# A recurrent attention layer and a routed feed-forward layer in one kernel: gates of the first 256 steps ahead, routing cut into small pieces, weights and q loaded in other portions

## The chip, the core and the metric

The kernel runs on one core of a Trainium2 chip. The core has five engines that each work through an instruction list of their own: TensorE (PE in the rows; its weight loads are PEld), VectorE (DVE), ScalarE (ACT), GpSimd (POOL) and SyncE (SP), which here only issues DMAs. The lists are joined by semaphores. SBUF is the on-chip memory, PSUM takes the results of the matrix unit. The metric is the time of one execution on the device in microseconds (us), as the median of repeated runs.

## The reference

Two layers stand one behind the other. The first is an mLSTM cell with an exponential input gate, which the reference runs step by step:

```python
for t in range(S):                         # B, H, S, D = 4, 8, 768, 40
    m_new = np.maximum(f_gate[:, :, t] + m, i_gate[:, :, t])
    f_stab = np.exp(f_gate[:, :, t] + m - m_new)
    i_stab = np.exp(i_gate[:, :, t] - m_new)
    m = m_new
    C = f_stab * C + i_stab * (v_t outer k_t)      # D x D
    n = f_stab * n + i_stab * k_t
    y[:, :, t] = sigmoid(o_gate[:, :, t]) * (C @ q_t) / max(|n . q_t|, 1)
```

Its rows become a table of 3072 rows of 320 numbers. The second layer sends each row to one of 8 experts, chosen by its token number alone (`token * 2654435761 % 8`), and computes `relu(x @ w1[e]) @ w2[e]` with 1024 hidden units. All numbers are f32.

## The kernel before

**Attention.** The 768 steps of a batch are six blocks of 128 steps. One pass of the main loop is one block of one batch: pass `s` is block `c = s % 6` of batch `b = s // 6`, 24 passes in all (called passes here, to keep them apart from the reference's steps). A prologue computes the gates of all steps of all batches: a running maximum over the 768 steps (`gates`, one scan), then decays within each block, each split into three bf16 pieces, written to a DRAM scratch table and read back per block: `load_a(s)` brings the decay pieces into one of two tiles `R`, `load_e(b)` the input pieces of a whole batch into one of two tiles `L`. A pass then does, on TensorE, in this order:

- `turn_k(s + 2)`: transposes k of the pass after the next (L285); `turn_q(b + 1, r)`: transposes sixths of q of the NEXT batch (L301): one sixth at c = 0, two at c = 1, one each at c = 2, 3, 4, none at c = 5, none in the last batch. ahead of each, `pad_q` copies that sixth into a padded tile `qp` on VectorE (L293)
- `decays(s + 1)`: outer sums of gate pieces (`ab` L316, `xb` L324), which ScalarE turns into weights `w` by Exp
- `state(s)` (L382), `scores(s + 1)` (`sp`, L353), which VectorE multiplies into `w` (L357)
- `attend(s)`: rows of the output in `xh` (L396 with the carried state `C`, L401 with `w`). VectorE then takes the denominators `den`; the next pass multiplies them with the output gate on GpSimd (`gated`, `og`), finishes the rows (`finish`, `x`) and stores them

SP issues the loads of a pass ahead of it: k and v of three passes ahead, `load_a(s + 2)`, the output gates, q of a whole batch at once (`load_q`, tile `ql`, 960 KB), and the store of x, which waits for VectorE in the middle of a pass. SP's list is worked off in order, so what stands behind a wait is late too.

**Routing.** Ranks and slots of the tokens per expert need VectorE, a little TensorE and GpSimd. They are independent of the attention and are spread over it by a dictionary: `pieces[s]` runs at the end of pass s, behind `attend(s)`. `route_slots` is one piece (after pass 5), and `route_table` makes one-hot tables of six token columns on VectorE (`oh_c`, `oh_r`) and GpSimd and at once multiplies them on TensorE (`tk`, L544), after passes 6 to 9. `load_weights(e)` of the first three experts (2.5 MB each) are pieces too, after passes 12, 14 and 16.

**Experts.** When the last row is stored, GpSimd gathers rows by expert (L629), TensorE transposes them (L649, L651) and runs layer 1 (L666, L673) and layer 2 (L702) of each expert in turn; outputs are scattered to DRAM. The weights of expert e + 3 are loaded behind expert e.

## Time and profile before

| | |
|---|---|
| median of 3 runs | 499.65 us (499.44 to 501.44) |
| profiled execution | 499.33 us, of which the span of the core is 497.6 us |
| mean granted TensorE clock in the span | 0.912 of full speed |
| TensorE, VectorE, ScalarE, GpSimd busy | 421.3, 148.7, 129.8, 112.1 us |

The profiled execution lies 0.3 us below the median. Its span is the time from the first to the last recorded instruction; some 1.7 us lie around it. A busy time is a mean over a prologue, 24 passes and 8 experts, which are limited by different things, so the table alone doesn't tell what an edit is worth. In the rows a time in square brackets is the idle time of that engine just before the instruction, and the name behind the arrow is what ended it. SPq and ACTq rows are DMA issues by SP and ScalarE. The granted clock is given as a share of 2.4 GHz: 1.00 is that level throughout, 0.5 would be 1.2 GHz throughout.

### The profile page before, as it was taken

The numbers are of one execution on the slowest core, as the hardware profiler recorded it, in microseconds if no ns is written. First come the engines' busy times: TensorE is split into PE (matmuls) and PEld (weight loads), VectorE is DVE, ScalarE is ACT, GpSimd is POOL, SyncE is SP. The second block draws the span as 40 slices with busy tenths as digits, with TensorE's granted clock in tenths as the row PEclk, the third lists the DMA queues.
The fourth block names the chain that finished last, engine by engine and source line by source line (L and its number), as shares of the span: only waits on it lengthen the run. The fifth ranks groups of instructions, "written<-read, shape, count | busy, mean of one in ns | idle before, by whom it ended". The sixth has DMA issues, their size and how long they took to land.

```text
span 497.6 us, 6769 instructions
## 1 busy us (share of the span) xinstructions
PE 421.3 (85%) x2604; PEld 297.2 (60%) x2604; DVE 148.7 (30%) x379; ACT 129.8 (26%) x221; POOL 112.1 (23%) x176
## 2 busy tenths in 40 slices
PE   0288885888895789799399999999999999999993
PEld 0167773777784678688156656565565656656552
DVE  6525657444463354365211020201102011110100
ACT  4795541121442444133011111111111111111100
POOL 3106211222212221142521402313122131102011
PEclk9999976677787898799589999999999999999997
DMA  7374447222346988731314417271331710001000
GB/s 183 78 168 85 98 81 178 42 43 44 68 95 177 240 251 234 176 73 41 90 55 135 143 23 228 67 235 56 119 125 51 232 60 13 26 0 39 1 13 28
DMA packets 103642, 50.94 MB, mean 102 GB/s; under 512 B 79572, under 2 KB 99896, under 8 KB 103608
## 3 DMA queue, kind: packets, MB, share of 16 engines
q1 hardware_dynamic: 100392, 41.59, 32.8%
q0 software_dynamic: 2496, 8.20, 5.2%
q10 hardware_dynamic: 720, 0.70, 0.5%
q8 instruction: 21, 0.34, 0.3%
q14 instruction: 13, 0.11, 0.1%
HBM read 42.07 MB, written 8.63 MB: 102 GB/s over the span
## 4 chain that ended last, share of the span: by engine, by line
PE 69%; issue 10%; DMA 8%; DVE 6%; POOL 3%; ACT 2%; SPq 1%; POOLq 0%; ACTq 0%; DVEq 0%
PE mh L673 19%; PE zp L702 18%; PE mh L666 5%; PE xh L401 5%; PE sp L353 4%; PE xh L396 3%; PE ab L316 3%; PE tr L301 3%; DMA R<-gate_pieces 2%; PE xh L382 2%; PE tk L544 2%; PE tr L285 2%; DMA k<-in_k_dram 2%; DMA ql<-in_q_dram 1%; PE tp L649 1%
## 5 line engine op out<-in xcount | busy, mean ns | idle before, releaser
L702 PE MATMUL zp<-w2t,h 128*128 128x320 f32 x384 | 105.2, 433 | 0.0
L673 PE MATMUL mh<-xT,w1t 128*128 128x416 f32 x256 | 98.2, 528 | 0.9 <-issue 0.9
L702 PEld LDWEIGHTS zp<-w2t,h 128*128 128x128 f32 x384 | 72.7, 190 | 32.1 <-issue 3.3
L673 PEld LDWEIGHTS mh<-xT,w1t 128*128 128x128 f32 x256 | 47.6, 194 | 43.9 <-issue 42.8
L401 PE MATMUL xh<-v,w 128*128 128x41 f32 x384 | 54.1, 275 | 0.0
L655 DVE COPY xT<-tp 128x384 f32<-128x384 f32 x16 | 8.9, 557 | 141.7 <-PE tp L651 124.0
L401 PEld LDWEIGHTS xh<-v,w 128*128 128x128 f32 x384 | 49.8, 193 | 0.7 <-issue 0.4
L636 POOL DMA_INDIRECT out_dram<-zo,s_idx x26 | 25.6, 985 | 92.6 <-ACT zo L635 92.6
L682 ACT ACTIVATE h<-mh 128x416 f32<-128x416 f32 x32 | 16.5, 517 | 109.5 <-PE mh L666 59.6
L286 ACT COPY kT<-tr 128x512 f32<-128x512 f32 x24 | 14.0, 584 | 101.9 <-PE tr L285 101.9
L635 ACT COPY zo<-zp 128x320 f32<-128x320 f32 x26 | 11.1, 425 | 101.1 <-PE zp L702 92.9
L301 PE MATMUL tr<-ident,qp 128*128 128x128 f32 x96 | 20.9, 368 | 17.0 <-DVE qp L293 15.0
L680 DVE TENSOR_SCALAR h<-mh 128x416 f32<-128x416 f32 x32 | 18.9, 591 | 53.4 <-PE mh L673 26.9
L396 PE MATMUL xh<-C,qs 128*128 128x82 f32 x160 | 34.7, 299 | 0.0
L357 DVE TENSOR_TENSOR w<-sp,w 128x512 f32<-128x512 f32 x48 | 30.8, 683 | 11.1 <-PE sp L353 9.7
L353 PE MATMUL sp<-qT,kT 64*128 64x128 f32 x384 | 32.3, 315 | 0.0
L302 ACT COPY qT<-tr 128x512 f32<-128x512 f32 x24 | 25.2, 1092 | 17.6 <-PE tr L301 17.6
L413 POOL TENSOR_TENSOR og<-og,den 128x320 f32<-128x320 f32 x24 | 17.4, 724 | 54.6 <-DVE den L410 43.8
L353 PEld LDWEIGHTS sp<-qT,kT 64*128 64x128 f32 x384 | 27.5, 217 | 2.9 <-issue 0.4
L301 PEld LDWEIGHTS tr<-ident,qp 128*128 128x128 f32 x96 | 14.9, 186 | 21.1 <-issue 16.9
L328 DVE TENSOR_TENSOR qs<-qT,xb 128x512 f32<-128x512 f32 x20 | 13.8, 688 | 44.5 <-PE xb L324 44.5
L666 PE MATMUL mh<-xT,w1c 64*128 64x416 f32 x128 | 26.7, 535 | 0.0
(158 smaller groups left out, 429.1 us busy)
## 6 DMA issues: line engine op xcount, KB each, us to landing
w2t<-in_moe_w_dram SPq DMA_DIRECT2D x8, 1280.0 KB
w1t<-in_moe_w_dram SPq DMA_DIRECT2D x8, 1024.0 KB
ql<-in_q_dram SPq DMA_DIRECT2D x4, 960.0 KB
k<-in_k_dram SPq DMA_DIRECT2D x24, 160.0 KB
v<-in_v_dram SPq DMA_DIRECT2D x24, 160.0 KB
og<-in_o_gate_dram SPq DMA_DIRECT2D x24, 160.0 KB
x_rows<-x SPq DMA_DIRECT2D x24, 160.0 KB
w1c<-in_moe_w_dram SPq DMA_DIRECT2D x16, 128.0 KB
```

Of the source, the lines that this page charges most:

```text
L301: nc.tensor.transpose(tp[:, j, :], t[:, 2 * j : 2 * j + 2, :].rearrange("p h d -> p (h d)"), ident[:])
L302: nc.scalar.copy(qb[b]["T"][:, :, r::NB], tp[:])
L353: nc.tensor.matmul(sp[hf][:, j, :], lhsT=d["kT"][r, j, :], rhs=q_of(s)[r, j, :], start=True, stop=True,)
L357: nc.vector.tensor_tensor(d["w"][:, hf], sp[hf][:], d["w"][:, hf], op=ALU.mult)
L396: nc.tensor.matmul(d["xh"][:, 2 * j * D1 : (2 * j + 2) * D1], lhsT=d["qs"][:, j, :], rhs=st["C"][:, j].rearrange("p h d -> p (h d)"), star ...
L401: nc.tensor.matmul(hs[:, 2 * j + hf, :], lhsT=d["w"][:, hf, j, :], rhs=d["v"][:, 2 * j + hf, :], start=(c == 0), stop=True, skip_group_che ...
L413: nc.gpsimd.tensor_tensor(og[s], og[s], st[s]["den"][:].to_broadcast([P, H, D]), op=ALU.mult)
L636: ins = nc.gpsimd.indirect_dma_start(out=out[:, :], out_offset=bass.IndirectOffsetOnAxis(ap=idx, axis=0), in_=zo[:], in_offset=None, bound ...
L666: nc.tensor.matmul(hp[i][:, :cols], lhsT=w1c[r, fp, :], rhs=xT[r, 2, :cols], start=first, stop=not first,)
L673: nc.tensor.matmul(hp[i][:, :cols], lhsT=w1t[:, db, fb * P : (fb + 1) * P], rhs=xT[:, db, :cols], start=(first and db == 0), stop=(not fir ...
L680: nc.vector.tensor_relu(h[:, 2 * fp, :cols], hp[i][:, :cols])
L702: nc.tensor.matmul(zp[:], lhsT=h[:, fb, j * P : (j + 1) * P], rhs=w[2][:, fb, :], start=(fb == 0), stop=(fb == FB - 1),)
```

## The change

- **Gates in two parts.** The first 256 steps (32 rows, blocks 0 and 1 of every batch) are computed straight from the first third of the scan, without the copy into the layout `mP`; the other 512 steps (64 rows) behind the scores of pass 0. `gates` writes the decay and input pieces, `gates_rest` the exponentials. Each now writes two scratch tables, `za_d` and `ze_d`, on SP. Part of the copies is on GpSimd.
- **Tables.** Only one `R` and one `L` are built; the other of each pair is filled by a DMA from the first, ahead of `load_a(0)` and `load_e(0)`.
- **q.** q of batch 0 is loaded by blocks (`load_q0`, 160 KB each), two in the prologue, the rest in passes 0 to 2, and transposed in the prologue and passes 0 to 3. `load_q(1)` is issued in pass 0. For the other batches `pad_q` for the next pass stands at the end of a pass, ahead of `attend`, in four tiles `qp` instead of two.
- **Routing.** The work is cut into pieces of one to five VectorE instructions that stand ahead of `attend` in passes 2 to 19; the one-hot tables are of three columns, made a pass ahead of their matmuls.
- **Weights.** Ten DMAs per expert; those of experts 0 and 1 go one per pass in passes 3 to 12 and 13 to 22, expert 2 is loaded when the gathers are issued.
- **Order of the loads in a pass.** k, (q), R, v, (L), (q of a batch), output gates, weight slice; R used to be behind v.

```diff
-    wpool = ctx.enter_context(tc.tile_pool(name="wpool", bufs=3))
-    w2pools = [ctx.enter_context(tc.tile_pool(name="w2pool", bufs=3))]
+    wpools = [ctx.enter_context(tc.tile_pool(name="wpool", bufs=2))]
+    w2pools = [ctx.enter_context(tc.tile_pool(name="w2pool", bufs=2))]
...
+        parts = [
+            (t[:, db, f0 : f0 + F // 2], s1[:, db, f0 : f0 + F // 2])
+            for t in (w1t,) for db in range(2) for f0 in (0, F // 2)
+        ]
+        parts += [(w1c[i * P // 2 : (i + 1) * P // 2], last[i]) for i in range(2)]
+        parts += [(w2t[:, fb : fb + 2, :], s2[:, fb : fb + 2, :]) for fb in range(0, FB, 2)]
+        return (w1t, w1c, w2t), [lambda d=d, r=r: nc.sync.dma_start(d, r) for d, r in parts]
...
+    def weight_slices(e):
+        W[e], slices = weights(moe_w1[e], moe_w2[e], wpools[e % 3 // 2], w2pools[2 <= e < 6])
+        return slices
...
-        qps = [gp.tile([P, H, DP], F32, name=f"qp{i}") for i in range(2)]
+        qps = [gp.tile([P, H, DP], F32, name=f"qp{i}") for i in range(4)]
...
+        def load_k(s):
+            st[s] = {"k": ks[s % NK], "v": vs[s % NK]}
+            nc.sync.dma_start(ks[s % NK][:, :, :D], rows_of(k, s))
+        def load_v(s):
+            nc.sync.dma_start(vs[s % NK][:, :, :D], rows_of(v, s))
...
+        def load_e(b, gs):
+            src = ze_d.rearrange("(g b h) i t -> b (h i) g t", g=NC2, h=H)[b]
+            nc.sync.dma_start(
+                Ls[b % 2][: 3 * H, :].rearrange("r (g t) -> r g t", t=W2)[:, gs[0] : gs[-1] + 1],
+                src[:, gs[0] : gs[-1] + 1],
+            )
...
+        def gates(rows, m0, m1, f, i, engs):
+            r = rows
+            first = r.start == 0
+            nc.vector.tensor_add(aP[r], f, m0)
+            nc.vector.tensor_sub(aP[r], aP[r], m1)
+            if first:
+                nc.vector.memset(aP[r, 0:1], 0.0)
+            nc.gpsimd.tensor_tensor(iP[r], i, m1, op=ALU.subtract)
+            nc.vector.tensor_tensor_scan(AP[r], keep[r], aP[r], 0.0, op0=ALU.mult, op1=ALU.add)
+            def copies(z, i0, t, ra, rb, eng):
+                for j, piece in enumerate((hi(t[r]), hi(ra[r]), rb[r])):
+                    (eng.copy if eng is nc.scalar else eng.tensor_copy)(z[r, i0 + j, :], piece)
+            nc.vector.tensor_tensor(r1[r], AP[r], hi(AP[r]), op=ALU.subtract)
+            nc.vector.tensor_sub(iP[r], iP[r], AP[r])
+            nc.vector.tensor_tensor(r2[r], r1[r], hi(r1[r]), op=ALU.subtract)
+            copies(zA, 0, AP, r1, r2, engs[0])
+            nc.vector.tensor_tensor(r3[r], iP[r], hi(iP[r]), op=ALU.subtract)
+            nc.vector.tensor_tensor(r4[r], r3[r], hi(r3[r]), op=ALU.subtract)
+            copies(zE, 0, iP, r3, r4, engs[1])
+            zr = slice(0, BH) if first else slice(BH, 3 * BH)
+            nc.sync.dma_start(za_d[zr, :3, :], zA[r, :3, :])
+            nc.sync.dma_start(ze_d[zr], zE[r])
...
+        def gates_rest(rows, eng):
+            r = rows
+            first = r.start == 0
+            zr = slice(0, BH) if first else slice(BH, 3 * BH)
...
+            nc.scalar.activation(aP[r], aP[r], AF.Exp)
+            nc.scalar.activation(fP[r], AP[r], AF.Exp)
...
+            for j, piece in enumerate((hi(fP[r]), hi(r1[r]), r2[r])):
+                (eng.copy if eng is nc.scalar else eng.tensor_copy)(zA[r, 3 + j, :], piece)
+            nc.sync.dma_start(za_d[zr, 3:, :], zA[r, 3:, :])
...
+            t = qb[b][r] = qps[2 + r % 2]
...
+        def load_q0(c):
+            t = qb.setdefault(0, {})[c] = qps[c % 2]
+            nc.sync.dma_start(t[:, :, :D], rows_of(q, c))
+        def turn_q0(c):
+            turn_q(0, c, slice(c * P, (c + 1) * P))
...
-        pieces = {
-            1: [route_consts], 3: [route_counts], 4: [route_extra], 5: [route_slots],
-            6: [lambda: route_table(0)], 7: [lambda: route_table(1)], 8: [lambda: route_table(2)],
-            9: [lambda: route_table(3)], 10: [route_index],
-            12: [lambda: load_weights(0)], 14: [lambda: load_weights(1)], 16: [lambda: load_weights(2)],
+        before = {
+            0: [lambda: iota_consts(0, 3)], 1: [lambda: iota_consts(3, 8)], 2: [route_consts, route_sel],
+            3: [route_ranks], 5: [route_extra1], 6: [route_extra2], 7: [route_rank],
+            8: [lambda: route_beyond(NM, rmoff)], 9: [lambda: route_beyond(CAP, b2)], 10: [route_slots],
+            11: [route_split], **{12 + i: [lambda i=i: route_hot(i)] for i in range(NT // TH)},
         }
+        after = {4: [route_counts], **{13 + i: [lambda i=i: route_table(i)] for i in range(NT // TH)}}
+        after[12 + NT // TH].append(route_index)
...
+        load_k(0)
+        load_q0(0)
+        load_k(1)
+        load_q0(1)
...
+        g0, g1 = slice(0, BH), slice(2 * BH, 4 * BH)
+        nc.vector.tensor_tensor_scan(
+            m_sb[:, 1 : W2 + 1], f_sb[:, :W2], i_sb[:, :W2], NEG, op0=ALU.add, op1=ALU.max,
+        )
+        turn_k(0)
+        turn_q0(0)
+        turn_k(1)
+        turn_q0(1)
+        gates(g0, m_sb[:, :W2], m_sb[:, 1 : W2 + 1], f_sb[:, :W2], i_sb[:, :W2], (nc.gpsimd, nc.scalar))
+        nc.sync.dma_start(Rs[1][:], Rs[0][:])
+        nc.sync.dma_start(Ls[1][:], Ls[0][:])
         load_a(0)
-        load_e(0)
-        load(2)
-        for r in range(NB):
-            pad_q(0, r)
-            turn_q(0, r)
+        load_e(0, [0])
...
+        for i, eng in ((1, nc.scalar), (2, nc.scalar)):
+            for t, src in ((fP, f_gate), (iP, i_gate)):
+                eng.dma_start(t[at[i] : at[i] + BH, :], src.rearrange("b h s -> (b h) s")[:, i * W2 : (i + 1) * W2])
+        nc.vector.tensor_tensor_scan(
+            m_sb[:, W2 + 1 :], f_sb[:, W2:], i_sb[:, W2:], m_sb[:, W2 : W2 + 1], op0=ALU.add, op1=ALU.max,
+        )
+        for i in (1, 2):
+            nc.scalar.dma_start(mP[at[i] : at[i] + BH, :], m_sb[:, i * W2 : (i + 1) * W2 + 1])
+        gates_rest(g0, nc.gpsimd)
         nc.scalar.dma_start(tok[:], moe_token_ids.rearrange("(p t) -> p t", t=NT))
-        turn_k(0)
-        turn_k(1)
+        load_k(2)
+        load_q0(2)
+        load_v(1)
         load_a(1)
-        load_q(1)
+        for s in range(3):
+            load_o(s)
+        load_v(2)
         decays(0)
         k_weights(0)
+        scores(0)
         sigmoid(0)
-        scores(0)
+        gates(g1, mP[g1, :W2], mP[g1, 1:], fP[g1], iP[g1], (nc.gpsimd, nc.scalar))
+        gates_rest(g1, nc.gpsimd)
+        load_e(0, [1, 2])
...
+        slices = []
         for s in range(NT):
             b, c = s // NB, s % NB
             if s + 3 < NT:
-                load(s + 3)
+                load_k(s + 3)
+                if b == 0 and c < 3:
+                    load_q0(c + 3)
             if s + 2 < NT:
                 load_a(s + 2)
+            if s + 3 < NT:
+                load_v(s + 3)
+            if c == 3 and b + 1 < B:
+                load_e(b + 1, [0, 1, 2])
+            if s == 0:
+                load_q(1)
+            if c == 5 and b + 2 < B:
+                load_q(b + 2)
...
+            if s in (3, 13):
+                slices += weight_slices(s // 10)
+            if slices:
+                slices.pop(0)()
...
+            if b == 0 and c < 4:
+                turn_q0(c + 2)
             if b + 1 < B:
                 for r in turns_of.get(c, ()):
-                    pad_q(b + 1, r)
-                    turn_q(b + 1, r)
+                    if r not in qb[b + 1]:
+                        pad_q(b + 1, r)
+                    turn_q(b + 1, r, slice(r, None, NB))
...
+            nb = b + (c == NB - 1)
+            if nb + 1 < B and s + 1 < NT:
+                for r in turns_of.get((c + 1) % NB, ()):
+                    pad_q(nb + 1, r)
+            for piece in before.get(s, []):
+                piece()
             attend(s)
...
-    w2pools.append(ctx.enter_context(tc.tile_pool(name="w2late", bufs=3)))
+    wpools.append(ctx.enter_context(tc.tile_pool(name="wlate", bufs=1)))
+    w2pools.append(ctx.enter_context(tc.tile_pool(name="w2late", bufs=4)))
...
         fetch(0)
         fetch(1)
+        load_weights(2)
         for piece in turns(0):
```

Two places of the instruction lists. The first is SP's list from the prologue into pass 0, with k_84 the k of block 2 and ql the q of batch 1. Before:

```order
L176 DMA R_99<-gate_pieces 3x8x128 x2
L165 DMA L_96<-gate_pieces 8x3x256 x3
L142 DMA k_84<-in_k_dram 128x8x40
L142 DMA v_88<-in_v_dram 128x8x40
L176 DMA R_100<-gate_pieces 6x8x128 x2
L161 DMA ql<-in_q_dram 128x8x240
L142 DMA k_85<-in_k_dram 128x8x40
L142 DMA v_89<-in_v_dram 128x8x40
```

After, from the scratch tables of the later 512 steps on:

```order
L226 DMA decay_pieces<-zA 64x768
L227 DMA input_pieces<-zE 64x768
L245 DMA decay_pieces<-zA 64x768
L186 DMA L_98<-input_pieces 24x2x256
L161 DMA k_85<-in_k_dram 128x8x40
L278 DMA qp_91<-in_q_dram 128x8x40
L197 DMA R_101<-decay_pieces 6x8x128 x2
L164 DMA v_89<-in_v_dram 128x8x40
L182 DMA ql<-in_q_dram 128x8x240
```

The load of batch 1's q stood ahead of pass 0 and behind no part of the gates but the first; now it stands behind all three stores of the later gates and behind the read of R that needs them.

The second place is VectorE's list, from the end of pass 5 into pass 6 before: the last ten of the instructions between the denominators of pass 5 and the work of pass 6.

```order
L513 TENSOR_TENSOR slot<-slot,gx 128x192
L514 TENSOR_TENSOR slot<-slot,b1off 128x192
L515 TENSOR_TENSOR slot<-slot,sel 128x192
L519 TENSOR_REDUCE sl<-slot 128x24
L520 CAST sl_i<-sl 128x24
L521 TENSOR_SCALAR rc_i<-sl_i 128x24
L522 TENSOR_SCALAR rc_i<-sl_i 128x24
L523 CAST rc<-rc_i 128x48
L293 COPY qp_90<-ql 128x8x40
L328 TENSOR_TENSOR qs<-qT,xb 128x512
```

After, the end of pass 8, where the part of this work for one capacity stands:

```order
L335 TENSOR_TENSOR w<-sp_1101,w 128x512
L335 TENSOR_TENSOR w<-sp_1102,w 128x512
L264 COPY qp_92<-ql 128x8x40
L501 TENSOR_SCALAR gx<-rank 128x192
L502 TENSOR_TENSOR gx<-gx,rmoff 128x192
L503 TENSOR_TENSOR slot<-slot,gx 128x192
L386 TENSOR_SCALAR den<-xh 128x8
L387 TENSOR_TENSOR den<-den,xh 128x8
L388 RECIPROCAL den<-den 128x8
```

The copy into qp, for which TensorE's transposes wait, used to be behind the routing work and in the pass that needs it; now it is ahead of the routing work and in the pass before, and the routing work stands ahead of the denominators.

## Rows read from the trace of the kernel before

**Rows 1.** Waits of PE between 31 and 237 us: total, times, longest.
```profile
PE tr L301 <- DVE qp L293: 13.8, 8, 6.2
...
PE tk L544 <- POOL oh_c L535: 9.6, 4, 2.4
...
PE tr L285 <- DMA k<-in_k_dram: 7.5, 3, 3.1
```
**Rows 2.** Timeline of PE: start, duration, instruction, merged; pass boundaries and waits.
```profile
33.08 0.66 PE L285 MATMUL tr<-ident,k 128*128 128x128 f32 x4
...
34.92 0.63 PE L301 MATMUL tr<-ident,qp 128*128 128x128 f32 x4 [1.18 <-DVE qp L293]
...
39.63 0.63 PE L285 MATMUL tr<-ident,k 128*128 128x128 f32 x4
...
72.60 0.64 PE L285 MATMUL tr<-ident,k 128*128 128x128 f32 x4
...
77.51 0.63 PE L285 MATMUL tr<-ident,k 128*128 128x128 f32 x4
...
84.34 1.09 PE L301 MATMUL tr<-ident,qp 128*128 128x128 f32 x4 [6.20 <-DVE qp L293]
...
89.58 1.98 PE L401 MATMUL xh<-v,w 128*128 128x41 f32 x16
...
93.95 2.79 PE L544 MATMUL tk<-oh_c,oh_r 128*128 128x47 f32 x12 [2.40 <-POOL oh_c L535]
...
216.11 0.63 PE L285 MATMUL tr<-ident,k 128*128 128x128 f32 x4
...
221.68 0.63 PE L285 MATMUL tr<-ident,k 128*128 128x128 f32 x4
...
234.63 0.57 PE L401 MATMUL xh<-v,w 128*128 128x41 f32 x4
```
**Rows 3.** Windows: PE, PEld, DVE, ACT, POOL busy, granted clock, DMA share, GB/s.
```profile
100.00:140.00 40.00, 32.82 (x274) 28.53 (x272) 16.86 (x42) 13.66 (x21) 9.11 (x11) 0.75 0.24 49
...
211.00:232.00 21.00, 21.00 (x255) 18.71 (x254) 13.62 (x35) 9.76 (x18) 7.13 (x10) 1.00 0.25 59
```
**Rows 4.** Timeline of all engines, prologue and pass 0.
```profile
3.80 1.75 DVE L242 TENSOR_TENSOR_SCAN m_sb<-f_sb,i_sb 32x768 f32<-32x768 f32 x1 [2.89 <-DMA f_sb<-in_f_gate_dram]
...
3.88 1.71 POOL L211 TENSOR_SCALAR_AFFINE_SELECT tri<-tri 64x64 f32<-64x64 f32 x1
...
15.07 0.42 DVE L258 TENSOR_TENSOR aP<-fP,mP 96x256 f32<-96x256 f32 x1 [1.87 <-DMA mP<-m_sb]
...
18.16 0.32 ACTq L256 DMA_DIRECT2D gate_pieces<-zt  x1
...
20.10 0.65 SPq L176 DMA_DIRECT2D R<-gate_pieces  x2
...
25.24 0.39 SPq L161 DMA_DIRECT2D ql<-in_q_dram  x1
...
33.13 1.28 ACT L345 ACT_TABLE_LOAD   x1
...
34.43 1.00 ACT L345 ACTIVATE og<-og 128x960 f32<-128x960 f32 x1
```
**Rows 5.** Chain that ended last, in order of time: start, duration, what.
```profile
146.22 7.06 DMA ql<-in_q_dram
...
161.29 9.25 DMA k<-in_k_dram
...
244.08 3.28 DMA xr<-x_rows,g_idx
```
**Rows 6.** Timeline of DVE inside the routing work behind pass 5.
```profile
79.27 0.66 DVE L511 TENSOR_SCALAR gx<-rank 128x192 f32<-128x192 f32 x1
...
80.75 0.26 DVE L511 TENSOR_SCALAR gx<-rank 128x192 f32<-128x192 f32 x1
```
**Rows 7.** Timeline of POOL at the same time.
```profile
79.08 0.73 POOL L338 TENSOR_TENSOR kw<-k,kw_T 128x320 f32<-128x320 f32 x1
```

More of the change, by code (lines that the diff above doesn't have):

```diff
@@ L85, with weights @@
     xe = consts.tile([1, NX + 1], I32, name="xe")
-    def weights(src1, src2, w2pool):
+    def weights(src1, src2, wpool, w2pool):
         w1t = wpool.tile([P, 2, F], F32, name="w1t")
@@ L446, with iota_consts, route_consts @@
         tv = gp.tile([P, NC], F32, name="tv")
-        def route_consts():
-            for ti, tf, pattern, base, mult in iotas.values():
+        def iota_consts(lo, hi_):
+            for ti, tf, pattern, base, mult in list(iotas.values())[lo:hi_]:
                 nc.gpsimd.iota(ti[:], pattern=pattern, base=base, channel_multiplier=mult)
                 nc.gpsimd.tensor_copy(tf[:], ti[:])
+        def route_consts():
             nc.gpsimd.memset(lt_strict[:], 1.0)
@@ L541, in route_table @@
             )
+        def route_table(i):
+            oh_r, oh_c = oh.pop(i)
             tk = ps.tile([P, NC], F32, name="tk", tag="tr", bufs=2)
@@ new lines @@
+        nc.scalar.dma_start(f_sb[:], f_gate.rearrange("b h s -> (b h) s"))
+        nc.scalar.dma_start(i_sb[:], i_gate.rearrange("b h s -> (b h) s"))
+        make_identity(nc, ident[:])
+        for t in [ks[0], qps[0], ks[1], qps[1]]:
+            nc.gpsimd.memset(t[:, :, D:], 0.0)
+        load_k(0)
+        load_q0(0)
+        load_k(1)
+        load_q0(1)
+        nc.vector.memset(m_sb[:, 0:1], 0.0)
+        tables()
+        for t in [ks[2], *kws, *qps[2:], ks[3]]:
+            nc.gpsimd.memset(t[:, :, D:], 0.0)
@@ L617 @@
                 scores(s + 1)
+            nb = b + (c == NB - 1)
[3 more added lines that the diff above has]
+            for piece in before.get(s, []):
+                piece()
             attend(s)
-            for piece in pieces.get(s, []):
+            for piece in after.get(s, []):
                 piece()
@@ L783 @@
             nc.vector.tensor_copy(gs[:, 1:2], s_idx[:, bass.ds(k + (NC - NX), 1)])
-            w = weights(
+            w, slices = weights(
                 moe_w1[bass.ds(ex, 1)].rearrange("e d f -> (e d) f"),
-                moe_w2[bass.ds(ex, 1)].rearrange("e f d -> (e f) d"), w2pools[0],
+                moe_w2[bass.ds(ex, 1)].rearrange("e f d -> (e f) d"), wpools[0], w2pools[0],
             )
+            for piece in slices:
+                piece()
             xr = xp.tile([P, DB * P], F32, name="xr")
```

259 lines of the change are left out of this document (103 added, 156 removed).

## The prediction

> **What bounds the kernel now.** I read TensorE's waits first, then its timeline, then windows and the chain. Between the prologue and the experts TensorE stands idle for three causes: 13.8 us for a padded sixth of q, 9.6 us for one-hot tables, 7.5 us for k [rows 1]. The timeline shows the price of one such stop: in pass 6 the padded q comes 6.20 us late, and the matmuls behind the stop run slower, 1.09 us for the four transposes that take 0.63 us elsewhere [rows 2]. The windows say why: between 211 and 232 us TensorE is busy all the 21 us at a granted clock of 1.00 (2.4 GHz), between 100 and 140 us, where three of the four table stops lie, it is granted 0.75 on average, a mix with 1.2 GHz [rows 3]. So a stop costs its length and then a stretch at half clock. Where nothing stops it, TensorE itself sets the pass: 5.57 us (216.11 to 221.68) [rows 2]. The chain names the loads: q of batch 3 takes 7.06 us from issue to landing, and a k that was issued behind expert weights 9.25 us [rows 5]. Ahead of pass 0 (33.08) it is a chain of small operations and DMAs that counts [rows 2, 4].
>
> The 24 passes take 33.08 to 235.2 us (234.63 + 0.57) [rows 2], 202 us, 8.4 us each. That is where the change works; the experts behind it keep their instructions.
>
> **The start, and q of batch 1.** Now the issue of ql for batch 1 is at 25.24 [rows 4], and its first sixth is needed at 34.92 [rows 2]. After, it stands on SP behind everything of the later gates, so I follow that chain.
>
> - The scan of 768 columns takes 1.75 us from 3.80 [rows 4]; a third is 0.6. i_gate is now second on ScalarE's list, so I let the scan end at 5. Three operations of 0.42 us (the row of 96x256; the time goes with the columns, and they stay 256) and a short scan bring the decays to 6.9. GpSimd must first fill pads and tables, among them the affine_select of 1.71 us [rows 4]; I put its subtraction at 8 to 8.5. Three more operations on VectorE and three copies on ScalarE at about 0.42: the input pieces are stored at 10.5.
> - The copies of R and L to their second tiles (0.7 MB) follow on SP, and `load_a(0)` overwrites the source, so it waits until they have landed. At the rate of ql (0.98 MB in 7.06 us [rows 5]) that is 5 us: 15.5. A small DMA needs 1.94 us until its reader can go on (18.16 to 20.10 [rows 4]): pass 0's decays at 17.5, some 14 us earlier than now.
> - Scores and their products occupy PE and VectorE until 22, the later gates on VectorE (ten operations of 0.42) until 26. ScalarE meanwhile has the sigmoid with its table load in front (1.28 + 1.00 [rows 4]), and it waits for output gates that SP issues only behind the first exponentials' round trip, landed at about 24. So its copies of the input pieces end at 27, then again a table load of 1.28 and two exponentials of 0.42: 29. Two subtractions, a GpSimd copy: the last store is issued at 30.5, read at 32.4.
> - Two reads of R and v (0.65 + 0.5): ql is issued at 33.6 and, by 7.06 us, lands at 40.7. The copy and the hand-over: TensorE's q transposes of pass 0 at **41.3**, against 34.92.
>
> So the early gates give nothing back; pass 0 ends later. Bounds of this term: 37 (ScalarE never waits for the output gates) and 46 (GpSimd's and VectorE's operations get in each other's way).
>
> **The passes.** TensorE has idled, so the rest of pass 0 goes at low clock, as pass 6 does now from 84.34 to 91.56 (89.58 + 1.98) [rows 2]: 7.2 us. Pass 1 begins at 48.5 (now 39.63). At full clock, with 5.57 as base and 0.63 per turn of q [rows 2], and no wait for the pad, since it is made a pass ahead: pass 1 with two turns and one of batch 0 takes 7.5, passes 2 and 3 (two turns) 6.8, pass 4 with the counts 6.8, pass 5 takes 4.9 (72.60 to 77.51). Pass 6 begins at 81.3 (now 77.51).
>
> At pass 6 the stop stays, with another cause. q of batch 2 is still issued in pass 5, some 0.6 us into it (77.0), lands at 84.0, is padded at 84.4: transposes at 84.5, now 84.34. Half of the stop of now was hidden behind routing; what is late next is the load. With 7.2 us, pass 6 ends at 91.7. **Up to here nothing is gained**, and this is the checkpoint of the forecast.
>
> Then: now a table stop follows (2.40 us, twelve matmuls of 2.79 in sum [rows 2]), and three more. After: pass 7 takes 6.8, passes 8 to 10 take 6.2 each, pass 11 takes 4.9: pass 12 begins at 122. q of batch 3 is issued at 117.7, so 125.3 + 7.2: pass 13 at 132.5. Passes 13 to 17: 6.8 + 3 x 6.2 + 4.9 = 30.3; the 24 table matmuls that lie in passes 13 to 20 at 0.12 each (half of 2.79/12): 2.8. Pass 18 begins at 165.6. It has no turn: 39.63 - 33.08 - 1.18 - 0.63 = 4.74. Pass 19 takes 5.57, passes 20 to 23 as now 19.1 (216.11 to 235.2) [rows 2]: the last row is done at **195.0** instead of 235.2, **-40.2**.
>
> The weights no longer come in bursts: a slice of 256 KB per pass is a quarter of a pass's traffic, so k and R should arrive in time; the stops of 7.5 us for k [rows 1] are in the sum as gone.
>
> Added: (a) routing ahead of `den`. VectorE is busy 13.62 of 21 us at full clock [rows 3], 3.6 of 5.57; the routing behind pass 5, at most 6.20 us [rows 2], in five parts is 1.2 each. 5.1 us fit into a pass of 6.2, so the work is covered; without the cover it would add up to 0.7 a pass. I take 2.5 us over all passes, with 0 and 14 as ends. (b) Expert 2's weights travel while the first gathers do: one of them lands 3.28 us after issue now, and the worst load behind weights took 9.25 [rows 5], so 0 to 6; I take 1.5, since the two use different queues. The later experts' loads have the whole time of an expert's matmuls and cost nothing.
>
> Sum: -40.2 + 2.5 + 1.5 = -36.2, against the profiled 499.3: **463.1 us**; that execution lies 0.3 us under the median of the three runs, so 463 it stays.
>
> A rule that speaks against the change: when the routing operation `gx` runs beside a GpSimd multiplication it takes 0.66 us, and 0.26 us alone [rows 6, 7]. The Trainium skill, page "SBUF — State Buffer", section "Who interferes with whom", says that VectorE and GpSimd share a port pair which one instruction holds to its end while the other one blocks; the rows agree. If that lock met the routing in every pass, the sum would be that of the second rival below, 475; where it meets it now and then, the 2.5 us of (a) hold it.
>
> **The rivals.**
> 1. *The start pays.* If the later gates need 8 to 12 us less than I count (GpSimd's and ScalarE's orders interlock more kindly), ql is issued near 23 and pass 0 doesn't stop. Then pass 1 begins near 36 instead of 48.5; only the distance up to the q stop of pass 6 moves, and that moves along: -12, **451**. For it: the first scan is a third as long. Against it: three stores and three round trips in a row.
> 2. *VectorE becomes the bound.* Each of some 20 passes with routing or pads loses 0.4 us twice (0.66 - 0.26 [rows 6]): VectorE at 5.9 plus waits, passes of 6.9 instead of 6.2. Price: 0.7 x 20 less the 2.5 counted, **475**. It decides from 1.5 us of routing a pass on. For it: rows 6 and 7. Against it: the parts are short and GpSimd is busy 7.13 of 21 us [rows 3].
> 3. *Slower: the DMA engines become the bound.* Between 100 and 140 us they are 0.24 busy at 49 GB/s [rows 3], so some 204 GB/s when full with such rows. A pass moves 640 KB for k, v, gate and x, 160 KB of q and a slice: 1.08 MB, 5.3 us of 6.2. If short rows and slices slow each other to below 129 GB/s, a pass takes 8.4 us, as now, and with the later start the kernel ends near **507**. It decides below that rate. Against it: 211 to 232 us moves little, and bytes are fewer than now by one expert.
> 4. *The waits only move.* R or k is late in every pass as behind the weights now, and a clock that falls again each time keeps the passes at 8 us or more: within 2 us of now.
>
> **How the numbers follow.** Chances: forecast 0.58 (own range 455 to 472, from the bounds of the start and of the additions), the start pays 0.15, VectorE 0.20, DMA-bound 0.05, waits only move 0.02. The predicted time is the forecast's, 463. To leave out no more than 2 in 10, the range takes in rival 2 with half its reach beyond and part of rival 1: 446 to 481. Faster by over 0.5% (what a measurement of this kernel can tell from no change) is everything but the last two: 0.93; the same 0.02; slower 0.05.
>
> **What would show it.** Right: PE's first `ab` near 17 us, then a stop of 10 us or more in pass 0 that ends with qp, whose ql was issued behind the second read of R; stops of 2 to 3 us at passes 6 and 12 named qp or ql; no wait for oh_c and none for k; granted clock 1.00 between passes 7 and 11 and from 13 on; last attend near 195 us; experts unchanged in length. Wrong: pass 6 reached long before 80 us (rival 1); passes of 6.9 us with PE waiting for VectorE at full clock (rival 2); PE waiting for k, v or R, or a DMA share above 0.9 through the passes (rivals 3 and 4).

## The result, and the profile after

The changed kernel takes 468.6 us (median of 4 runs, 464.8 to 473.5), the kernel before beside it 500.5 us: 0.934 of the time, interval 0.924 to 0.944. Measured once more it took 469.4 us (6 runs, 461.5 to 472.1; ratio 0.925, 0.917 to 0.933). 463 us was forecast, with a range from 446 to 481. Medians hold every execution, ratios and intervals only those within 1.5% of the fastest of their kernel. Between the two measurements of this one kernel the ratio moves by 0.009, some 4.5 us, so smaller differences are not read from the times alone. The profiled execution (473.45 us, span 471.7 us) lies at the upper end of this spread, because TensorE was granted half clock in it from 190 us to the end of the passes; a later look at the same kernel (466.35 us, span 464.6 us) shows full clock there, so what is said of passes 22 and 23 is read from that one.

TensorE's waits after the change, from 31 to 220 us, answer to [rows 1]. The 9.6 us for one-hot tables and the 7.5 us for k are gone. What is left for q is one long wait in pass 0 and one short one each in passes 6 and 12 (the latter is named sl_i, a routing result; VectorE's timeline, and an experiment below, show that it was the load), and one ahead of the experts, for the first gathered rows (12.6 us, 8.1 before). Short waits for ScalarE's copy of the transposed k (`kT`) add up to 2.9 us (1.5 before).

```profile
PE tp L739 <- DMA xg<-x_rows,g_idx: 12.6, 1, 12.6
PE tr L272 <- DVE qp L264: 10.9, 2, 9.2
```

TensorE's timeline after the change, at the places of [rows 2]: the first decays, the q transposes of pass 0, the beginnings of passes 1, 6 and 7 with the stop between, the same around pass 12, and the end.

```profile
17.23 1.07 PE L295 MATMUL ab<-R,L 128*64 128x512 bf16 x4 [2.41 <-DMA L<-input_pieces]
...
42.47 1.09 PE L272 MATMUL tr<-ident,qp 128*128 128x128 f32 x4 [9.21 <-DVE qp L264]
...
49.29 0.64 PE L259 MATMUL tr<-ident,k 128*128 128x128 f32 x4
...
82.34 0.64 PE L259 MATMUL tr<-ident,k 128*128 128x128 f32 x4
84.63 1.03 PE L272 MATMUL tr<-ident,qp 128*128 128x128 f32 x4 [1.66 <-DVE qp L264]
...
90.85 0.63 PE L259 MATMUL tr<-ident,k 128*128 128x128 f32 x4
...
120.73 0.63 PE L259 MATMUL tr<-ident,k 128*128 128x128 f32 x4
123.68 1.09 PE L272 MATMUL tr<-ident,qp 128*128 128x128 f32 x4 [2.32 <-DVE sl_i L515]
...
130.81 0.64 PE L259 MATMUL tr<-ident,k 128*128 128x128 f32 x4
...
204.97 0.99 PE L379 MATMUL xh<-v,w 128*128 128x41 f32 x4
218.57 0.66 PE L739 MATMUL tp<-ident,xg 128*128 128x128 f32 x2 [12.60 <-DMA xg<-x_rows,g_idx]
```

Pass 0 now starts its decays at 17 us and then stands until 42.47 us, 7.55 us later than before. Behind the two stops the matmuls run slow (1.03 and 1.09 us for four transposes, 0.63 us elsewhere). In between the clock is full, as the windows show: TensorE is busy the whole 24 us from 96 to 120 us at 1.00, and from 100 to 140 us it is granted 0.91 where it was 0.75 [rows 3].

```profile
96.00:120.00 24.00, 24.00 (x270) 21.73 (x269) 17.23 (x48) 13.81 (x21) 7.47 (x11) 1.00 0.71 160
100.00:140.00 40.00, 37.39 (x388) 32.76 (x386) 25.82 (x75) 19.42 (x33) 11.91 (x18) 0.91 0.76 173
```

SP's timeline says why pass 0 stands: q of batch 1 (`ql`) is issued behind the reads of the late gates, 10.7 us later than before [rows 4].

```profile
34.53 0.89 SPq L197 DMA_DIRECT2D R<-decay_pieces  x2
...
35.92 0.57 SPq L182 DMA_DIRECT2D ql<-in_q_dram  x1
```

VectorE's timeline says what the wait of pass 12 is: VectorE itself stands 3.50 us for the load `ql` ahead of the copy into `qp`, and `sl_i` is only the next instruction in its list, at 123.45.

```profile
123.21 0.33 DVE L264 COPY qp<-ql 128x320 f32<-128x320 f32 x1 [3.50 <-DMA ql<-in_q_dram]
```

At the other end, the chain that ended last runs from the last store of x (SPq L397) through a slice of expert 2's weights to the first gather. The gather needs the rows of that store, and the store stands between these slices in SP's list.

```profile
207.96 0.32 SPq L397
...
208.32 3.78 DMA w1t<-in_moe_w_dram
...
212.37 5.89 DMA xg<-x_rows,g_idx
```

Before, the chain held the last store of x, the first gather and the first product of an expert in these places:

```profile
237.20 1.74 DMA x_rows<-x
...
240.08 1.18 POOL xg L629
...
249.27 3.14 PE mh L673 x4
```

The first product began 14.1 us behind the end of attention (234.63 + 0.57 [rows 2]). In the later look at the changed kernel it is 17.6 us; its timeline of TensorE:

```profile
82.19 0.63 PE L259 MATMUL tr<-ident,k 128*128 128x128 f32 x4
...
188.02 0.45 PE L374 MATMUL xh<-C,qs 128*128 128x82 f32 x2 [0.63 <-DVE C L366]
...
198.11 0.58 PE L379 MATMUL xh<-v,w 128*128 128x41 f32 x4
211.47 0.66 PE L739 MATMUL tp<-ident,xg 128*128 128x128 f32 x2 [12.78 <-DMA xg<-x_rows,g_idx]
...
216.33 5.35 PE L763 MATMUL mh<-xT,w1t 128*128 128x416 f32 x8 [0.90 <-POOL xT L825]
```

So the 33.0 us between the spans (497.6 and 464.6) split like this:

| stretch | before | after (later look) | difference |
|---|---|---|---|
| up to the start of pass 6 | 77.51 | 82.19 | +4.7 |
| passes 6 to 23 | 157.69 | 116.50 | -41.2 |
| end of attention to the first expert product | 14.07 | 17.64 | +3.6 |
| experts, to the end of the span | 248.3 | 248.3 | 0 |

### The profile page after: what moved, and what is told of

Its sections match the earlier page's. It is cut to its first block, busy times and chain, and to the rows that moved or that the text cites. A ratio compares the mean times of both kernels' runs of the same rounds, so it can differ in the third digit from the quotient of the medians.

```text
span 471.7 us, 6898 instructions
## 1 busy us (share of the span) xinstructions
PE 409.7 (87%) x2606; PEld 289.2 (61%) x2606; DVE 145.3 (31%) x390; ACT 120.3 (26%) x213; POOL 120.4 (26%) x200
## 4 chain that ended last, share of the span: by engine, by line
PE 77%; DMA 9%; issue 5%; DVE 3%; ACT 2%; SPq 1%; POOL 1%; ACTq 1%; POOLq 0%; DVEq 0%
PE mh L763 20%; PE zp L792 19%; PE xh L379 9%; PE mh L756 5%; PE sp L331 5%; PE xh L374 5%; DMA ql<-in_q_dram 4%; PE ab L295 3%; PE tr L272 2%; PE xh L360 2%; PE tr L259 2%; PE tp L739 1%; DMA xg<-x_rows,g_idx 1%; PE xb L303 1%; PE tk L544 1%
## 5 line engine op out<-in xcount | busy, mean ns | idle before, releaser
L379 PE MATMUL xh<-v,w 128*128 128x41 f32 x384 | 57.6, 286 | 0.0
L379 PEld LDWEIGHTS xh<-v,w 128*128 128x128 f32 x384 | 53.5, 205 | 0.6 <-issue 0.2
L374 PE MATMUL xh<-C,qs 128*128 128x82 f32 x160 | 36.9, 314 | 0.6 <-DVE C L366 0.6
L725 ACT COPY zo<-zp 128x320 f32<-128x320 f32 x26 | 11.1, 425 | 101.1 <-PE zp L792 92.9
L770 DVE TENSOR_SCALAR h<-mh 128x416 f32<-128x416 f32 x32 | 18.9, 591 | 53.4 <-PE mh L756 26.5
L335 DVE TENSOR_TENSOR w<-sp,w 128x512 f32<-128x512 f32 x48 | 30.8, 682 | 10.7 <-PE sp L331 9.0
L272 PE MATMUL tr<-ident,qp 128*128 128x128 f32 x96 | 17.6, 316 | 17.1 <-DVE qp L264 10.9
L331 PEld LDWEIGHTS sp<-qT,kT 64*128 64x128 f32 x384 | 26.5, 210 | 3.1 <-issue 1.6
L374 PEld LDWEIGHTS xh<-C,qs 128*128 128x128 f32 x160 | 26.1, 205 | 3.1 <-DVE C L366 0.8
L273 ACT COPY qT<-tr 128x512 f32<-128x512 f32 x24 | 22.9, 982 | 18.7 <-PE tr L272 18.7
L299 ACT ACTIVATE w<-ab 128x512 f32<-128x512 f32 x48 | 26.6, 610 | 3.9 <-PE ab L295 3.9
```

What stands on the lines that cost most here:

```text
L272: nc.tensor.transpose(tp[:, j, :], t[:, 2 * j : 2 * j + 2, :].rearrange("p h d -> p (h d)"), ident[:])
L273: nc.scalar.copy(qb[b]["T"][:, :, cols], tp[:])
L299: nc.scalar.activation(w[:, hf], ab[:], AF.Exp)
L331: nc.tensor.matmul(sp[hf][:, j, :], lhsT=d["kT"][r, j, :], rhs=q_of(s)[r, j, :], start=True, stop=True,)
L335: nc.vector.tensor_tensor(d["w"][:, hf], sp[hf][:], d["w"][:, hf], op=ALU.mult)
L374: nc.tensor.matmul(d["xh"][:, 2 * j * D1 : (2 * j + 2) * D1], lhsT=d["qs"][:, j, :], rhs=st["C"][:, j].rearrange("p h d -> p (h d)"), star ...
```

## The experiments

All are edits of the changed kernel; none leaves work out. The medians, with the ratio to the kernel before, run beside each:

| kernel | median us | runs, us | ratio, interval |
|---|---|---|---|
| unaltered, again | 469.4 | 461.5 to 472.1 | 0.925, 0.917 to 0.933 |
| q of batch 1 early | 454.3 | 450.0 to 462.2 | 0.901, 0.894 to 0.907 |
| expert 2's weights later | 464.2 | 456.4 to 468.8 | 0.915, 0.908 to 0.923 |
| routing at its old places | 486.1 | 485.1 to 486.5 | 0.968, 0.961 to 0.975 |
| list of rows later | 468.6 | 467.0 to 470.7 | 0.933, 0.928 to 0.938 |
| q of batches 2 and 3 early | 459.4 | 457.8 to 461.6 | 0.913, 0.909 to 0.918 |
| weights in bursts | 468.0 | 465.6 to 471.1 | 0.932, 0.926 to 0.937 |
| no padding ahead | 476.9 | 471.4 to 484.2 | 0.945, 0.938 to 0.952 |
| pieces behind attention | 467.0 | 463.7 to 471.7 | 0.932, 0.927 to 0.936 |
| three edits together | 445.0 | 444.2 to 446.2 | 0.886, 0.883 to 0.889 |
| three edits and the later list | 444.3 | 443.3 to 446.6 | 0.885, 0.882 to 0.888 |

**The unaltered kernel again.**

> The changed kernel once more, unaltered. The profile shown with its result has the clock at half level from about 190 us to the end of the passes, and its time, 473.45 us, is the longest of four. Theory A: the low clock of the last passes belongs to that execution; a median near 465 us, and in a profile at 465 us the last attend ends near 198 us with the granted clock at 1.00 until then. Rival: the last passes always run at half clock; then about 470 us, and the last attend ends near 206 us in every profile.

The time is the same within what these runs can tell, and the half clock at the end stood in this profile too. That spoke for the rival and left the question open; it is taken up below.

**q of batch 1 early.**

```diff
         load_v(2)
+        load_q(1)
         decays(0)
...
-            if s == 0:
-                load_q(1)
```

> The load of batch 1's q is issued in the prologue, behind the third load of v and ahead of the stores of the later gates; nothing else is changed. Theory A (the early gates gain nothing because this load stands behind the later gates): ql is issued near 22.5 us and lands near 30 us, the transposes of pass 0 that now start at 42.5 us start near 33.5 us, every later pass moves along by 9 us, 456 us against 465. Rival (another load becomes the late one, since R and k of pass 1 are issued no earlier): PE waits in pass 1 for R, k or q of block 3, 3 to 5 us gained, 460 to 462 us.

15 us less in the medians, 12 by the ratios (0.901 against 0.925). In TensorE's timeline the q transposes follow at once, and pass 1 begins at 40.17 us:

```profile
32.32 1.97 PE L272 MATMUL tr<-ident,qp 128*128 128x128 f32 x8 [0.59 <-DVE kw_T L250]
...
40.17 0.64 PE L259 MATMUL tr<-ident,k 128*128 128x128 f32 x4
```

So the long wait of pass 0 was the place of this one load in SP's list. With it out of the way pass 1 begins 0.5 us later than before the change (39.63 [rows 2]): at that point the gates in two parts have gained nothing. (No run has the old gates beside the rest of the change.) The gain is larger than the 9.1 us by which pass 1 comes earlier. Against the later look, at full clock too, the span is 11.7 us shorter (452.9 and 464.6): 9.0 at pass 1, 1.4 in pass 6, whose wait falls from 1.22 to 0.94 us, 1.0 in pass 12. The medians' further 3 us are within the scatter of the unaltered kernel.

**Expert 2's weights later,** issued by ScalarE behind the transposes of the first gathered rows:

```diff
-        load_weights(2)
         for piece in turns(0):
             piece()
+        for piece in weight_slices(2):
+            piece(nc.scalar)
```

> The ten DMAs of expert 2's weights are issued by ScalarE behind the transposes of the first gathers, instead of by SP around the last two stores of x. Theory A (they hold up the last stores and share the queues with the gathers): from the end of the last attend to the first expert matmul 14 us as in the kernel before, instead of 17.5; minus 3.4 us, about 462 us. Rival (the gap is longer because PE is at low clock there, or the gathers are slower for another reason): the gap stays near 17 us and the time within 1 us of the changed kernel.

5 us less in the medians, but the intervals of the ratios overlap (0.915 and 0.925), so the profile has to show it. TensorE's timeline shows the wait for the first gather at 8.40 us in place of 12.60:

```profile
212.99 0.66 PE L739 MATMUL tp<-ident,xg 128*128 128x128 f32 x2 [8.40 <-issue]
...
218.70 5.39 PE L763 MATMUL mh<-xT,w1t 128*128 128x416 f32 x8 [0.90 <-POOL xT L825]
```

The last product of attention ends at 204.59 us in this profile, so the gap is 14.1 us, as before the change: the 3.5 us were this load.

**Routing at its old places,** in large pieces behind attention, the tables made in the pass that multiplies them:

```diff
-        before = { ... }
+        before = {}
...
+            1: [lambda: iota_consts(0, 8), route_consts], 3: [route_sel, route_ranks, route_counts],
+            4: [route_extra1, route_extra2],
+            5: [route_rank, lambda: route_beyond(NM, rmoff), lambda: route_beyond(CAP, b2), route_slots, route_split],
+            **{6 + i: [lambda i=i: tables_of(i)] for i in range(4)}, 10: [route_index],
```

> Undoes the routing part alone: the same instructions, but in the places of the kernel before, behind attend in passes 1, 3 to 10, with the one-hot tables made in the pass of their matmuls. Theory A (most of the gain is the table and count stops and the low clock behind each): PE waits 2 to 3 us behind passes 3 and 6 to 9, granted clock near 0.8 in passes 4 to 10; plus 20 to 25 us, about 487 us. Rival (the loads, weights and pads gave most of it): plus 10 us or less, 475 us.

17 us more in the medians, 20 between this profile (486.38) and the later look. The old stops are back in TensorE's waits: tables, the addition to C behind the routing of pass 5, the counts. In the timeline the four table stops (one shown) lie at the ends of passes 6 to 9, which take 17.2, 12.7, 12.0 and 11.2 us:

```profile
PE tk L544 <- POOL oh_c L532: 6.4, 4, 1.6
PE xh L379 <- DVE C L364: 4.5, 1, 4.5
...
PE cps L462 <- DVE pr L455: 2.4, 1, 2.4
```
```profile
100.83 2.80 PE L544 MATMUL tk<-oh_c,oh_r 128*128 128x47 f32 x12 [1.61 <-POOL oh_c L532]
```

**Pieces behind attention,** small as they are and in the same passes:

```diff
+            attend(s)
             for piece in before.get(s, []):
                 piece()
-            attend(s)
```

> One edit: the routing pieces keep their passes and sizes, but are put behind the attention of the pass, so behind the denominators in VectorE's list, not ahead of them. Theory A (the prediction's term a: ahead of the denominators they cost some 2.5 us over all passes, which this saves, while they are short enough to be hidden at the new place): 467 us, at most 3 us under the unaltered kernel's 469. Rival B (the place is what hides them: behind the denominators they stand ahead of the padding, the product with q and the addition to C of the next pass, and TensorE waits for these): 5 to 10 us more, 474 to 479 us, with longer waits for C, kw or qp on TensorE. Rival C: neither, 469 us, and only the size of the pieces matters.

467.0 us: against 468.6 and 469.4 that is no difference that these runs can tell. Theory A's 2 us are no more than these runs scatter. Waits of 3.4 us appear for `den`, but they are the waits for q of passes 6 and 12 under another name: there VectorE stands 2.76 and 3.04 us for `ql` ahead of its copy, and `den` is the next in its list. With the run ahead of it, this says that the gain of the routing lies in its pieces being small and spread and in the tables being made a pass ahead, which were not undone one by one, and that the place ahead of the denominators is worth no more than the scatter.

**q of batches 2 and 3 early.**

```diff
-            if c == 5 and b + 2 < B:
+            if c == 3 and b + 2 < B:
                 load_q(b + 2)
```

> One edit: the loads of q of batches 2 and 3 are issued two passes earlier (in the fourth pass of a batch, not in the sixth). Theory A: the waits for the padded q ahead of the q transposes in passes 6 (1.66 us) and 12 (2.32 us) are lateness of these loads; they go, with the slow clock around them (pass 6 takes 8.5 us, pass 12 10.1 us, their neighbours 5 to 7), together 4 to 8 us: 463 us. Rival B: these loads now stand ahead of k, v and o of the passes in SP's queue, and what is won at q is lost at k or at the output gate: 469 us, and the profile shows longer waits for k or for sl_i.

9 to 10 us less in the medians, 6 to 10 by the ratios (0.913 against 0.925 and 0.934). In TensorE's timeline passes 6 and 12 now take 5.11 and 5.12 us, where they took 8.51 and 10.08 us: 8.4 us in sum, more than the two waits of 4.0 us.

```profile
85.78 0.63 PE L259 MATMUL tr<-ident,k 128*128 128x128 f32 x4
...
90.89 0.63 PE L259 MATMUL tr<-ident,k 128*128 128x128 f32 x4
...
120.77 0.63 PE L259 MATMUL tr<-ident,k 128*128 128x128 f32 x4
...
125.89 0.63 PE L259 MATMUL tr<-ident,k 128*128 128x128 f32 x4
```

The wait named sl_i at pass 12 goes with the earlier load. That pass 6 ends here when it ends in the unaltered kernel is this execution's: its first passes were slower, the sixteen products of pass 0 took 3.63 us (1.98 in the unaltered profile), and pass 6 began 3.4 us later.

**Weights in bursts.**

```diff
-            if s in (3, 13):
-                slices += weight_slices(s // 10)
-            if slices:
+            if s in (12, 14):
+                slices += weight_slices((s - 12) // 2)
+            while slices:
                 slices.pop(0)()
```

> One edit: the weights of experts 0 and 1 are again issued in one burst each (in passes 12 and 14), not in one slice a pass from 3 on and from 13 on. Theory A (the prediction: the slices are what took the waits for k and R of passes 13 to 17 away): TensorE waits for k or R again in passes 13 to 16, 4 to 8 us, and the clock falls to 0.75 or less there: 479 us. Rival B: with q and the tables out of the way the bursts are hidden: 469 us. Rival C: the free queue in passes 3 to 11 saves something and the time is under 466 us.

468.0 us, as the unaltered kernel. But the profile shows A and C at once. TensorE's timeline has the stop for k back, and passes 13 and 14 take 18.9 us (126.91 to 145.82), in the unaltered kernel 14.4 (130.81 to 145.17). Ahead of that, without a slice in the queue, the stop of pass 6 is 0.97 us and its clock stays up, and pass 7 begins at 87.98 us and not at 90.85.

```profile
83.31 0.63 PE L272 MATMUL tr<-ident,qp 128*128 128x128 f32 x4 [0.97 <-DVE qp L264]
87.98 0.63 PE L259 MATMUL tr<-ident,k 128*128 128x128 f32 x4
...
126.91 0.63 PE L259 MATMUL tr<-ident,k 128*128 128x128 f32 x4
...
136.97 1.09 PE L259 MATMUL tr<-ident,k 128*128 128x128 f32 x4 [2.26 <-DMA k<-in_k_dram]
145.82 0.63 PE L259 MATMUL tr<-ident,k 128*128 128x128 f32 x4
```

So the slices do what they were credited with, 4.5 us in passes 13 and 14, and are paid for ahead of these: pass 13 begins 3.9 us earlier without them, of which 2.2 lie in pass 6, 1.0 in pass 12 and 0.6 already at the start, where no slice is issued yet. That they make q late is the likeliest way, from the shorter wait in pass 6; it wasn't tried apart.

**No padding ahead.**

```diff
-            nb = b + (c == NB - 1)
-            if nb + 1 < B and s + 1 < NT:
-                for r in turns_of.get((c + 1) % NB, ()):
-                    pad_q(nb + 1, r)
```

> One edit: q is padded in the pass that transposes it (as before the change), not one pass ahead. Theory A (the prediction: 18 turns of some 0.5 us each of TensorE waiting for the padded copy): 9 us more, 478 us, and the wait for qp ahead of the q transposes is back in every pass that has them. Rival B: the copies are done in time anyway, since VectorE or GpSimd reach them before TensorE does: 469 us.

7 to 8 us more in the medians, as theory A gives to within the scatter, though not by its working; attention ends 10.2 us later than in the later look (208.84 and 198.69). From 60 us on TensorE waits for qp seven times, five of them some 0.5 us, in all 5.7 us; the unaltered kernel waits 4.0 us there for q (1.66 + 2.32). About half of the price is clock: passes 12 to 14 take 29.7 us, in the later look 24.9, though TensorE waits no longer in pass 12 (2.14 and 2.87 us). The windows show it: 0.68 from 120 to 140 us and 0.90 behind it, in the later look at the unaltered kernel 0.83 and 1.00. Passes 8 to 10 take 0.7 us more each, at full clock.

```profile
120.00:140.00 20.00, 17.78 (x130) 14.85 (x129) 10.18 (x31) 5.56 (x10) 5.65 (x8) 0.68 0.86 195
140.00:160.00 20.00, 18.54 (x196) 15.52 (x195) 12.19 (x31) 8.31 (x16) 5.70 (x8) 0.90 0.36 85
```
```profile
120.00:140.00 20.00, 16.84 (x159) 14.10 (x160) 10.60 (x34) 7.19 (x13) 6.89 (x10) 0.83 0.77 171
140.00:160.00 20.00, 18.54 (x216) 16.60 (x210) 13.02 (x35) 11.44 (x17) 5.28 (x8) 1.00 0.57 125
```

**List of rows later.**

```diff
-        after[12 + NT // TH].append(route_index)
+        after[14 + NT // TH] = [route_index]
```

> One edit: the five VectorE rows that make the list of rows to gather (now between the attention of pass 20 and the addition to the state C of pass 21) are put behind the attention of pass 22. Theory A: these rows hold up the addition to C, TensorE stops there for 0.63 us at 188 us, and the half clock that follows until the last attend costs some 7 to 8 us in the executions of about 470 us; without them the profile shows no such stop, full clock from 180 to 200 us and a time of 462 us. Rival B: the half clock comes from elsewhere (it belongs to the execution, or to the stop itself being there already without these rows): the row of the half clock stays, and the time is 468 us, plus or minus 1.5.

The stop of 0.63 us and the half clock are both gone from the profile, and the median is 468.6 us all the same: the time speaks for B. (Its first passes were as slow as those of the run with q of batches 2 and 3 early, 3.63 us for the products of pass 0, and pass 6 begins 2.9 us later than in the later look; but from the start of pass 21 to the end of attention it takes 13.5 us and the later look 14.2, so the edit gains the stop and no more.) A third look at the unaltered kernel bears on the half clock.

> The changed kernel unaltered, a third profile. Both profiles so far show half clock from some 189 us to the end of the passes, and their executions lie at 472 and 473 us, at the upper end of a spread from 461 us on. Theory A (the half clock belongs to the execution, and the fast ones don't have it): if this execution is below 467 us, its profile has full clock from 180 to 200 us and the last attend ends 6 to 8 us earlier than 206. Rival B (the half clock belongs to this order of work): it is there whatever the time.

466.35 us, with full clock: the window from 180 to 200 us is at 1.00, the last attention ends at 198.69 us and not at 205.96, and the stop of 0.63 us stands there as ever (188.02, shown above). So the half clock doesn't belong to this order of work, and costs 7.3 us where it comes. What brings it on stays open; the looks were not all taken on one chip, so chip and execution are not told apart.

**Three edits together** (the diffs of q of batch 1, q of batches 2 and 3, expert 2's weights).

> Three edits at once: q of batch 1 is loaded in the prologue, q of batches 2 and 3 two passes earlier, and the weights of expert 2 are issued by ScalarE behind the transposes of the first gathered rows. Alone they measured 15, 10 and 5 us less than the unaltered kernel's 469. Theory A (three stops at three places, each with its own slow clock): the gains add up, 469 - 30 = 439 us. Rival B (the early q of batch 1 already took part of the stop of pass 6, and in the shifted passes loads of q, R and k crowd): 445 to 450 us.

445.0 us: rival B in the number. The gains, 30 us when added as medians, give 24; as ratios to the kernel before (0.925 less 0.901, 0.915 and 0.913) they add up to 23 us and give 20. The shared part shows in passes 6 and 12: q of batch 1 early already takes them from 18.6 us (later look) to 16.2, so that of the 8.4 us only 6.0 are left. No crowding of q, R and k shows. Between 40 and 180 us nothing is left to win from the clock:

```profile
40.00:180.00 140.00, 135.95 (x1520) 120.88 (x1519) 92.62 (x267) 70.61 (x116) 47.16 (x81) 1.00 0.70 156
```

With the list of rows moved as well:

> As the kernel with the three edits at once, and the five rows that make the list of rows to gather stand behind the attention of pass 22. Alone this measured nothing (468.6 against 469.4), though it took away a stop of 0.63 us in pass 21. Expected: the same as the three edits within 1 us; a gain of 0.6 us at most if the stop counts, a loss of up to 2 us if the later list delays the first gather.

444.3 us, the same. Both beat the changed kernel by some 24 us in the medians, 20 by the ratios.

## Why the prediction was right, point by point

- **The start** (pass 0's q transposes at 41.3, pass 1 at 48.5): 42.47 and 49.29 us. The reason given, that ql stands behind the reads of the late gates, is shown by the run that moves this one load. Rival 1 had priced a kernel whose ql goes out near 23 us at 451 us; with the load moved it is issued at 22.69 us, pass 1 begins at 40.17 and not near 36, and the median is 454.3.
- **The checkpoint** ("up to here nothing is gained"; pass 6 at 81.3, its transposes at 84.5, pass 7 at 91.7): 82.34, 84.63 and 90.85 us. The cause, a late load of q, holds too: loaded two passes earlier, the stop goes.
- **Passes 7 to 17** (pass 12 at 122, 13 at 132.5, 18 at 165.6): 120.73, 130.81 and 166.00 us. Without turns waiting, passes 8 to 10 take 6.0 us each (6.2 forecast).
- **The last row** (195.0): 198.7 us in the look at full clock. Here a term was mis-sized: 24 table matmuls at 0.12 us were counted, 2.8 us, but it is 48, six in each of eight passes at some 0.68 us a pass, 5.4 us. Not foreseen were the stop of 0.63 us, with routing rows ahead of the addition to C, and waits of 0.73 us for `kT` in passes 15 and 16, which take 7.6 us each where one turn and a table make 6.7; what makes `kT` late there was not tried.
- **Addition (a)**, 2.5 us for routing ahead of the denominators: moving the pieces behind them changes the median by no more than the scatter, so the term is neither confirmed nor refuted. The 5.1 us that were to fit into a pass are 4.8 by the terms given (3.6 + 1.2); it changes nothing.
- **Addition (b)**, expert 2's weights at 1.5 us (0 to 6): 3.5 us. The step named contention with the gathers alone. The profile shows that as half of it: from the start of the first gather to the first product it takes 11.1 us (212.37 to 223.43), 9.2 before (240.08 to 249.27). The other half is the last store of x, which stands among the slices: the gather starts 4.4 us behind its issue (207.96), 2.9 before.
- **The slices** were credited with the stops for k. They do remove one of them, 4.5 us in passes 13 and 14, but are paid for in passes 6 and 12, some 3 us, so that no gain is left that the medians can tell (468.0 without them). The step that left their price in passes 3 to 12 out is the one that failed here; it didn't show, because the stop of pass 6 was forecast from the load of q alone, and that came out right, in part by luck: without the slices the transposes start at 83.31 us, 1.3 earlier (0.6 of it from the start), and 84.5 was forecast.

The sum was -36.2 us; the look at full clock gives -33.0. Of the difference 0.9 us lies at the start (+4.7 at pass 6, +3.8 forecast) and 2.1 in (b). Passes 6 to 23 came out almost as forecast (-41.2, and -44.0 + 2.5 = -41.5), but in part by luck: pass 6 took 8.1 us and not 10.4, which makes up for most of the tables' 2.6 us, and (a)'s 2.5 us cover the waits that nobody counted. The medians lie 2 to 3 us above that look; in two profiles the clock fell at the end. The own range's upper end, 472, is not the sum of the bounds given (+4.7, +11.5 and +4.5, 484); the measured time lies below either.

**Rival 2** (VectorE the bound, 475) fell: passes of 6.0 us at full clock, TensorE busy without a gap from 96 to 120 us. The lock that the Trainium skill describes (page "SBUF — State Buffer", section "Who interferes with whom") is in this trace, and the engine that starts first goes through. At 23.39 us a GpSimd copy starts 0.03 us behind a subtraction of VectorE (23.36 us, 0.42 us long) and takes 0.65 us. At 30.35 us a copy of the same size starts 0.04 us ahead of one and takes 0.40 us, and VectorE's subtraction takes 0.64.

```profile
23.39 0.65 POOL L216 COPY zA<-AP 64x256 bf16<-64x256 bf16 x1 [5.43 <-DVE AP L211]
```
```profile
30.35 0.40 POOL L244 COPY zA<-fP 64x256 bf16<-64x256 bf16 x1 [4.89 <-ACT fP L240]
```
```profile
30.39 0.64 DVE L241 TENSOR_TENSOR r<-fP 64x256 f32<-64x256 f32 x1 [4.32 <-ACT fP L240]
```

The routing it meets seldom: both `gx` rows take 0.25 us, where [rows 6] showed 0.66 beside a GpSimd multiplication, because here they fall into times at which GpSimd waits (102.8 and 108.8 us). It does meet the list of rows, behind the attention of pass 20. In the profiled execution two of its rows run beside GpSimd multiplications (184.79 to 186.19 us) and take 0.53 and 0.65 us. Behind pass 22 the first of them runs alone and takes 0.14, and the last cast of the list, as large as the second row, takes 0.19 in either place. The 0.8 us or so that this costs stand ahead of the addition to C, for which TensorE stops 0.63 us.

```profile
185.02 0.53 DVE L553 TENSOR_SCALAR ta<-tv 128x47 f32<-128x47 f32 x1
185.58 0.65 DVE L554 CAST g_idx<-ta 128x47 int32<-128x47 f32 x1
```
```profile
197.33 0.14 DVE L553 TENSOR_SCALAR ta<-tv 128x47 f32<-128x47 f32 x1
```

**Rivals 3 and 4** fell with TensorE at full clock and no wait for k or R; the DMA share is 0.71 from 96 to 120 us.

Of the 41.2 us won in passes 6 to 23, the runs place some 16 in the routing (of the 20 between the profiles 4 lie in passes 3 and 4) and some 7 in the padding ahead. The rest, among it R loaded ahead of v, was not tried apart and stays open.

## What to carry to other kernels

When a load moves, read the queue's list and not the program's: one load of q behind three stores of gates cost 9 us at once and some 12 in all, and with it ahead of them the early gates just break even. A stop costs more than its length when the clock falls with it: 4.0 us of waiting for q in passes 6 and 12 cost 8.4. A wait's name can be an innocent one (sl_i and den here): look at what the named engine itself waited for, then move what is suspected and see whether the wait goes.

## What was not expected of the hardware

- Executions of one and the same kernel differ by 7.3 us at one place: from 190 us to the end of attention TensorE is granted half clock in some and full clock in others, though it was busy in both and stood 0.63 us just before in both. In the timeline of the profiled execution the sixteen score matmuls there take 2.08 us, in the later look 1.16.

```profile
193.50 2.08 PE L331 MATMUL sp<-qT,kT 64*128 64x128 f32 x16
```
```profile
192.04 1.16 PE L331 MATMUL sp<-qT,kT 64*128 64x128 f32 x16
```

- With all stops of 1 us and more gone from the passes (three edits together), the spread of the runs shrank from 10.6 us (461.5 to 472.1) to 2.0 us (444.2 to 446.2). The stops alone don't set it: with the list of rows moved and all of these stops left, it was 3.7 us.
